# Pieces of w1 and w2 loaded by threes, one ring buffer less, and a new order of all steps, in a delta-rule recurrence with a multiplicative feed-forward block

## The chip, the cores and the metric

The kernel runs on one core of a Trainium2 chip. The metric is the device time of one execution in microseconds (us). The core's engines are called as the profile calls them: PE (TensorE, matmuls; PEld is its weight load), DVE (VectorE), ACT (ScalarE), POOL (GpSimd) and SP (SyncE, which here only issues DMAs). Each engine works through its own instructions in a fixed order and waits on semaphores for the others. PE writes to PSUM banks of 128 x 512 float32, the other tiles lie in SBUF, 128 partitions wide.

## The reference

Two blocks follow each other. The first is a delta-rule recurrence over 768 tokens for 4 batches and 8 heads of 48, the second a feed-forward block with a product of two branches:

```python
B, H, S, D = q.shape                     # 4, 8, 768, 48
k_n = k / (np.linalg.norm(k, axis=-1, keepdims=True) + 1e-06)
for t in range(S):
    y[:, :, t] = np.einsum('bhd,bhde->bhe', q[:, :, t], state)
    v_old = np.einsum('bhde,bhd->bhe', state, kt)
    state = state + bt[:, :, :, None] * np.einsum('bhd,bhe->bhde', kt, vt - v_old)
x = y.transpose(0, 2, 1, 3).reshape(B * S, H * D)        # 3072 x 384
a = x @ w1                               # 384 x 1024
b = x @ w2                               # 384 x 1024
out = ((a * b) @ w3) @ w_out             # 1024 x 1024, 1024 x 384
```

q, k, v and beta are float32. The four weights lie in the chip's memory as float64, and the kernel turns them into float32 itself.

## The kernel before

**The recurrence.** The 768 tokens are cut into 12 chunks of 64, and the chunks are worked on in pairs u = 0 to 5. For a chunk m the kernel loads k, v and q, transposes keys and queries to channels by tokens (on PE, L368, or on DVE, L354), forms the scores of the tokens among themselves on PE (L450 and L456; for the chunks 0 and 1 L408 for the keys and L399 for the queries), multiplies them by masks on DVE (L419, L433), and inverts the triangular matrix U of a pair in 31 small steps on DVE (L523 and L528, with transposes before and after at L504 and L532). The inverse's corner blocks are then filled in by PE (L562, L601, L618, L645) with copies on ACT (L634). A chain of three short steps then carries the state from chunk to chunk: PE at L671, DVE at L705, L716, L735 and L737. The outputs y of a chunk are one more group of matmuls (L776), copied by ACT into the transposed activations xT (L794).

**The feed-forward block.** w3 and w_out are multiplied ahead of use: each 128-row piece of w3 is transposed on PE (L902), and PE folds it with w_out into a new 1024 x 384 weight (L911). For each pair of chunks PE then makes 8 products by w1 and 8 by w2 (L932), ACT copies the first (L944), DVE multiplies by the second (L948), and the result goes through the folded weight (L1164) with sums of slabs and of weights on POOL (L1005, L982) to the output (L1181 to L1199).

**The weights' pieces.** Weights come in 36 pieces: P0 to P7 are w_out (384 KB each), P8 to P23 the halves of w3 (512 KB), P24 to P29 w1 and P30 to P35 w2 (512 KB, 512 columns by 128 of 384 rows each; the first three of each weight are its first 512 columns). `piece` (L826 to L852) is a generator with four steps: SP issues the DMAs that bring the 64-bit words into a buffer called raw (L836); ACT turns the high and the low words into floats (L844, L847); DVE shifts the high part by three bits (L849); POOL adds the low part (L851). For w_out and w3 that is one DMA a piece. For w1 and w2 `piece_w12` hands over four sources, since the rows of a piece are spread in groups of 48 and 16 over the two halves of the partitions: 48 rows, 16 rows, 48 rows, 16 rows.

**Where the raw words lie.** raw is a ring of five tiles of 512 KB (`in_turn(ffn, ..., "raw", 5, ...)`): a piece that takes a turn waits until the piece five turns earlier is done with the tile. Pieces named in `GUESTS` (L814) take another place instead: the tiles kperm ("k") and qperm ("q"), which later hold permuted keys and queries (`load_perm`), or half of a spare tile that later holds KQ ("0" and "1"). After the last piece, `weight_sums` (step T) takes the five raw tiles and kperm for sums of weights.

**The order.** Nothing is scheduled by the program: each part is a generator, and `ORDER` is a string that names, token by token, whose next step is issued. `in_text_order` then fixes that each engine runs its instructions in exactly this order. So a step that is moved in the string moves on each engine on which it issues something, and an engine waits at its next instruction even if a later one could run. The names that matter here: `kN` loads k, `KN` and `QN` transpose keys and queries, `gN` squares of keys, `NN` their norms, `sN` scores, `hN` the first queries' scores, `VN` the inverse of a pair (V0 belongs to chunks 0 and 1), `eN` the corner of chunk N, `cN` the chain, `yN` the outputs, `PN` a piece, `tN` a transpose of w3, `fN` a fold, `aNM` and `bM` the products by w1 and w2, `T` the weight sums, `pN` the later loads of kperm and qperm. V0 and V1 keep one of the two double banks of PSUM called ps_w for as long as they run. `s0` and `s1` with their mask products make the four parts of U (L419, three at once and one more), after which V0 begins.

## Time and profile before

| | |
|---|---|
| time, median of 3 runs | 571.95 us (571.16 to 573.22) |
| the profiled execution's own time | 573.12 us |
| its span on the core | 571.4 us |
| granted PE clock, mean | 0.984 |
| busy: PE, DVE, POOL, ACT | 536.0, 349.1, 170.5, 144.7 us |
| moved by DMA | 54.22 MB, mean 95 GB/s |

The profile is one execution, so a sum of its parts stands against 573.12 us and not against the median. "Busy" is the time in which an engine computes; an instruction's row gives its start in the span, its duration, its engine, line and operation, the tile that it writes and those that it reads, their shapes, and in brackets how long the engine was idle before it and what ended that. Rows of like instructions that follow each other are put together, with their count (x64).

The slices of the page, 14.3 us each, show the stages. These are the DMA engines' busy share in tenths and the granted clock of PE:

```profile
PEclk9599899999999999999999999999999999999999
DMA  9988965549253465543594463164044313010001
```

The first five slices, 70 us, are those in which the weights' pieces and the first chunks are loaded; behind them lies the work that repeats for each pair.

### The profile page before, as it was taken

The page shows a single profiled execution, that of the slowest core. Times are in us where ns is not written, and L with a number is a line of the kernel's source. Part 1 is how long each engine was busy: PE and PEld are TensorE (multiplying, and loading weights), DVE is VectorE, ACT ScalarE, POOL GpSimd, SP SyncE. Part 2 cuts the span into 40 slices and gives each one's busy share as a digit, 9 for nine tenths or more (in the row PEclk, how much of TensorE's full clock was granted, in tenths as well). Part 3 has the DMA queues.
Part 4 walks back from the last instruction along what each step waited for, and adds up shares of the span by engine and source line. Part 5 has one row for each costly group of instructions (what it writes and reads, how often), then busy time and mean ns, then how long its engine had stood idle before and what let it go on. Part 6 is the DMA issues. An engine that isn't in the chain of part 4 may idle for free.

```text
span 571.4 us, 19958 instructions
## 1 busy us (share of the span) xinstructions
PE 536.0 (94%) x8732; PEld 391.1 (68%) x8732; DVE 349.1 (61%) x800; ACT 144.7 (25%) x291; POOL 170.5 (30%) x213
## 2 busy tenths in 40 slices
PE   4699897899999999998999999999999999989997
PEld 3556565788888644697544798444986446888897
DVE  6999754659735478755895624598355873123552
ACT  2776665331131011120111031110210102112210
POOL 6576046274361001614022160103522005621000
PEclk9599899999999999999999999999999999999999
DMA  9988965549253465543594463164044313010001
GB/s 225 294 302 194 184 141 122 136 90 116 63 75 67 78 131 90 82 78 75 90 134 88 62 95 72 53 96 88 15 68 92 69 39 55 18 57 1 0 2 55
DMA packets 191895, 54.22 MB, mean 95 GB/s; under 512 B 179296, under 2 KB 185440, under 8 KB 191808
## 3 DMA queue, kind: packets, MB, share of 16 engines
q1 hardware_dynamic: 189216, 52.46, 45.3%
q8 instruction: 68, 1.11, 0.8%
q10 hardware_dynamic: 2592, 0.49, 0.5%
q14 instruction: 19, 0.16, 0.1%
HBM read 41.78 MB, written 9.96 MB: 91 GB/s over the span
## 4 chain that ended last, share of the span: by engine, by line
PE 76%; DVE 14%; DMA 4%; issue 3%; ACT 2%; SPq 1%; ACTq 0%; DVEq 0%
PE ps_f L932 31%; PE ps_f L1164 20%; PE ps_w L671 5%; PE ps_w L776 4%; PE ps_f L1072 4%; DVE tb L523 3%; PE ps_w L618 3%; PE ps_f L911 3%; PE ps_w L1072 2%; DVE ps_w L528 2%; DVE Vb L528 2%; PE ps_w L450 1%; PE ps_w L456 1%; DVE TT L532 1%; DMA raw<-in_moe_w_dram 1%
## 5 line engine op out<-in xcount | busy, mean ns | idle before, releaser
L932 PE MATMUL ps_f<-xT,w1s 128*128 128x512 f32 (+1 forms) x288 | 107.3, 524 | 0.7 <-issue 0.6
L932 PE MATMUL ps_f<-xT,w2s 128*128 128x512 f32 (+1 forms) x288 | 107.0, 523 | 0.0
L1005 POOL TENSOR_TENSOR ab<-ab 128x256 f32<-128x256 f32 x80 | 56.2, 726 | 156.7 <-DVE ab L948 151.8
L932 PEld LDWEIGHTS ps_f<-xT,w1s 128*128 128x128 f32 x288 | 53.9, 190 | 47.1 <-issue 42.2
L932 PEld LDWEIGHTS ps_f<-xT,w2s 128*128 128x128 f32 x288 | 54.2, 190 | 45.8 <-issue 42.6
L1164 PE MATMUL ps_f<-w,ab 128*128 128x192 f32 x320 | 57.2, 332 | 2.0 <-DVE osb L1193 1.8
L944 ACT COPY ab<-ps_f 128x512 f32<-128x512 f32 (+1 forms) x48 | 23.7, 516 | 135.3 <-PE ps_f L932 135.3
L523 DVE TENSOR_TENSOR tb<-Vb,Ub 128x31 f32<-128x31 f32 (+15 forms) x124 | 43.7, 352 | 18.6 <-DMA Ub<-Ud 14.9
L1164 PEld LDWEIGHTS ps_f<-w,ab 128*128 128x128 f32 x320 | 51.6, 190 | 3.4 <-issue 2.5
L300 POOL TENSOR_TENSOR sq<-ktok 128x384 f32<-128x384 f32 x24 | 19.9, 831 | 91.8 <-DMA out_dram<-osb 54.6
L528 DVE TENSOR_TENSOR Vb<-Vb,tb 128x31 f32<-128x31 f32 (+15 forms) x124 | 44.0, 355 | 4.3
L911 PE MATMUL ps_f<-wo,w3T 128*128 128x384 f32 x128 | 45.4, 504 | 0.8 <-POOL wo L851 0.7
L1164 PE MATMUL ps_f<-room,ab 128*128 128x192 f32 x240 | 42.9, 332 | 0.0
L948 DVE TENSOR_TENSOR ab<-ab,ps_f 128x512 f32<-128x512 f32 (+1 forms) x48 | 27.5, 586 | 19.5 <-PE ps_f L932 19.5
L1164 PEld LDWEIGHTS ps_f<-room,ab 128*128 128x128 f32 x240 | 38.6, 190 | 0.9
L911 PEld LDWEIGHTS ps_f<-wo,w3T 128*128 128x128 f32 x128 | 24.0, 195 | 16.4 <-POOL wo L851 1.7
L634 ACT COPY T<-ps_w 32x512 f32<-32x512 f32 x24 | 13.8, 576 | 71.0 <-PE ps_w L618 69.0
L794 ACT COPY xT<-ps_w 112x256 f32<-112x256 f32 x48 | 14.3, 384 | 64.8 <-PE ps_w L776 64.8
L716 DVE TENSOR_TENSOR X<-ps_w,wt 128x768 f32<-128x768 f32 x12 | 11.5, 957 | 31.0 <-PE ps_w L671 23.8
L657 POOL TENSOR_TENSOR vtok<-vtok,n 128x384 f32<-128x384 f32 x24 | 20.4, 857 | 31.9 <-DVE KQ L354 15.3
L1193 DVE TENSOR_TENSOR room<-room,ps_f 128x384 f32<-128x384 f32 (+1 forms) x13 | 6.9, 533 | 26.8 <-PE ps_f L1164 26.8
L456 PE MATMUL ps_w<-KQ 48*64 48x64 f32 x640 | 22.6, 220 | 0.6 <-issue 0.6
(170 smaller groups left out, 810.9 us busy)
## 6 DMA issues: line engine op xcount, KB each, us to landing
vtok<-in_v_dram SPq DMA_DIRECT2D x24, 192.0 KB, 4.7
out_dram<-osb SPq DMA_DIRECT2D x46, 96.0 KB, 2.0
ktok<-in_k_dram SPq DMA_DIRECT2D x44, 96.0 KB, 3.8
raw<-in_moe_w_dram SPq DMA_DIRECT2D x8, 512.0 KB, 7.1
raw<-in_moe_w_dram SPq DMA_DIRECT2D x18, 192.0 KB, 4.6
raw<-in_moe_w_out_dram SPq DMA_DIRECT2D x7, 384.0 KB, 6.0
Ud<-U SPq DMA_DIRECT2D x40, 64.0 KB, 2.3
Ub<-Ud SPq DMA_DIRECT2D x5, 512.0 KB, 3.7
```

The lines of the kernel that those rows point to most:

```text
L456: pe.matmul(ps[half(z ^ j), 1, n + C * j : n + C * j + C], lhsT=x[:, 0, :], rhs=x[:, j, :], start=True, stop=True,)
L523: dve.tensor_tensor(out=tv, in0=V[:, 0 : s + 1, s : s + 1].to_broadcast([P, s + 1, n]), in1=U[:, s, s + 1 : BS].unsqueeze(1).to_broadcast( ...
L528: dve.tensor_tensor(out=o, in0=o, in1=tv, op=ALU.subtract)
L671: pe.matmul(out(ps, r, h, z), lhsT=lhs(r, h, z), rhs=rhs(r, h, z), start=True, stop=True,)
L776: i = pe.matmul(region(h, z, r), lhsT=lhs, rhs=rhs, start=part[n] not in part[:n], stop=part[n] not in part[n + 1 :],)
L911: pe.matmul(ps[:, 0:DM], lhsT=w3Ts[jc, kc // 4][:, kc % 4 * P : kc % 4 * P + P], rhs=wo(kc), start=(kc == 0), stop=(kc == KF - 1),)
L932: pe.matmul(ps[:].rearrange("p b c t -> p b (c t)"), lhsT=w[:, m, js], rhs=x[:, m, :, c0:c1].rearrange("p b c t -> p b (c t)"), start=(m = ...
L944: act.copy(out=t, in_=ps)
L948: dve.tensor_tensor(out=t, in0=t, in1=ps, op=ALU.mult)
L1005: (dve if u == last else pool).tensor_tensor(out=o_, in0=x_, in1=y_, op=op)
L1072: pe.matmul(ps[:, j, :], lhsT=w[j], rhs=x, start=first and j == 0, stop=j == 1, skip_group_check=not first,)
L1164: pe.matmul(ps[b][:, b, :], lhsT=ab_of(u, HF * f + i, t0), rhs=ws_[w][:, i], start=first and i == 0 and (b == 0 or n == "F"), stop=i == HF ...
```

## The change

Three things are done at once.

- w1 and w2 are loaded by threes. The three pieces that share their columns are loaded by the first of them with four DMAs (48 and 16 partitions, three rows of 4 KB each), and each piece converts its own third. The first half of w1 goes into the place of w2 (w2s, which is filled only later); the other three halves go through a new tile, `trio`, of three tiles' size.
- kperm and qperm become the first two thirds of `trio`. The ring of raw tiles has four instead of five, and `weight_sums` takes the last third of `trio` for the fifth. w1 and w2 pieces leave `GUESTS`; P16 is a guest of trio's last third ("t").
- `ORDER` is new from the first token to the last. Of its 47 lines the part up to the first step of e0 and somewhat behind it is shown, with the lines around the chain that are spoken of.

```diff
 ORDER = """
-k0 K0 g0 k1 g0 P8 g0 K0 K1 g0 beta K1 g0 P8 P1 P8 g0 P10 beta P12 g0 K0 P1 P9 P8 beta P12 P13 g0
-K1 P3 P1 g0 P1 P9 g0 P10 s0 N0 P0 P12 P13 P10 s1 P3 P12 P9 P13 q1 t4 s0 V0 s0 t0 s1 P3 P0 t0 P2 P4
-s1 P18 Q1 P10 V0 P0 P13 P9 t4 P3 P7 P2 V0 P6 t2 Q1 P2 t5 V0 Q1 V0 P5 V0 P4 P11 P0 P19 V0 t1 t2 q0
-P18 V0 P2 f2 P7 V0 P4 t5 P6 P5 P18 f0 V0 P7 t1 V0 P14 P6 h1 P19 V0 P4 P5 P17 P7 V0 V0 P6 P5 f2 P11
-V1 V0 P19 f0 V0 Q0 P16 P14 P11 P11 f0 V0 P22 f2 V0 V0 t3 P19 P23 P17 t3 V0 f1 P14 P18 f1 P16 h1 Q0
-P17 V0 t10 P15 V0 k2 Q0 P22 h1 V0 P17 k3 K0 f1 P16 V0 V0 t11 P23 V0 h0 P35 P20 P14 t10 P16 P28 N0
-t8 P23 P22 t11 t6 N0 f5 P15 f5 t8 V0 f5 P35 q2 V0 V0 V0 t6 V0 P15 V0 t9 f4 P22 P29 P23 h0 t14 t9
-V0 Q0 P26 f4 v0 V0 V0 V0 h0 t15 P27 g1 P15 P20 t14 t7 f4 Q2 V0 t15 V0 P20 Q2 t7 V0 P20 e0 n0 e0
-P28 Q2 P21 e0 e0 f7 K3 e1 e0 e0 e1 e1 P35 P26 f3 e0 P35 f3 P28 P29 P27 e1 P26 P29 q3 n0 P25 e1 c0
-c0 f7 P21 v1 P33 g1 g1 e1 f3 g1 c0 K3 f7 g1 P28 P30 e1 g1 P25 P21 P21 y0 y0 t12 y0 g1 c0 t13 g1 K3
-t13 P25 c1 P26 K2 n1 t12 f6 K2 K2 K0 P30 P33 n1 P34 Q3 g1 c1 P29 P27 g1 N1 P30 Q3 f6 k4 c1 c1 s2
-y0 P31 s2 s2 P27 f6 y1 Q3 P24 s3 s3 y1 P34 P25 b5 s3 P33 P34 P33 P31 s2 s3 b7 s2 g2 P31 b5 b4 s3
...
+k0 g0 K0 k1 g0 K0 g0 P8 K1 g0 P8 beta K1 K0 g0 K1 P0 g0 beta P9 V0 P8 g0 g0 P0 P12 g0 P2 P8 s1 P3
+q1 P0 beta P12 P2 P1 s0 g0 P10 P9 t0 N0 P2 P3 P12 P0 P9 t0 s1 P12 P5 P3 P1 Q1 N0 s0 s1 Q1 s0 P1 V0
+Q1 V0 P5 V0 V0 P2 V0 P5 V0 P3 V0 P1 P4 P13 t4 V0 P18 t4 P10 h1 N0 V0 P10 P13 P9 P4 t1 P5 P7 V0 P4
+t1 f0 P10 P7 t2 P13 P11 P6 P13 P16 t5 P4 P19 P18 P6 P11 V0 t5 P7 f2 V0 V0 P22 P7 P14 P19 P6 P23 V0
+P6 V0 P18 P18 f0 V0 f0 V0 P11 f2 V0 P17 V0 P11 t2 h1 P16 t3 t10 P16 V0 V0 P22 V0 t3 P17 P19 f1 V0
+V0 P19 q0 V0 P23 P22 f1 P16 f2 t10 f1 P23 V0 Q0 P15 k2 V0 P17 P22 Q0 V0 t11 V1 t11 V0 V0 V0 P15
+P14 P17 P23 Q0 t8 t8 f5 g1 P20 V0 V0 f5 P15 P14 h1 V0 V0 t9 t15 P15 P20 P24 V0 f5 t14 t9 P14 f4
+t14 t15 P25 f4 P24 q2 V0 t6 h0 P24 P21 t6 V0 Q2 f4 P21 Q2 e0 P24 e0 t7 v0 Q2 e0 P30 h0 P20 k3 h0
+f3 e0 P26 n0 P25 t7 n0 g1 K2 e1 e0 g1 e1 P26 P25 P31 P21 e0 P31 f7 P30 P26 K2 g1 e0 P31 f7 P30 e1
+g1 P32 c0 P32 e1 f3 g1 P30 c0 K2 v1 q3 P32 e1 c0 y0 P27 P21 f3 g1 P20 n1 t13 t12 y0 t12 g1 c0 c1
+y0 g1 g1 n1 t13 s2 c1 f7 K3 N1 y0 f6 e1 P29 P28 f6 k4 K3 P27 P29 P27 Q3 P28 K3 s2 e1 Q3 Q3 s2 P29
+P28 s2 s2 b2 s2 c1 P27 s3 f6 g2 c1 P33 g2 b7 y1 s3 u2 s3 s3 s3 u3 y1 P35 b7 y1 g2 b5 b2 b4 P34 T
...
-    kperm, qperm = (persist.tile([P, B, NP, 2, BS], FP32, name=x) for x in ("kperm", "qperm"))
+    trio = persist.tile([P, 3, B * NP * 2 * BS], FP32, name="trio")
+    kperm, qperm = (
+        trio[:, i].rearrange("p (b a x d) -> p b a x d", b=B, a=NP, x=2) for i in range(2)
+    )
...
-    GUESTS = {10: "k", 2: "0", 9: "q", 18: "1", 19: "k", 11: "q", 14: "0", 15: "1", 26: "k", 21: "q", 32: "k", 34: "q"}
+    GUESTS = {10: "k", 2: "0", 9: "q", 18: "1", 19: "k", 11: "q", 14: "0", 15: "1", 16: "t"}
...
-        if host in "kq":
-            x = {"k": kperm, "q": qperm}[host][:].rearrange("p b a x d -> p (b a x d)")
+        if host in "kqt":
+            x = trio[:, "kqt".index(host)]
...
-            raw = in_turn(ffn, [P, CW, 2], "raw", 5, "raw", U32)
+            raw = in_turn(ffn, [P, CW, 2], "raw", 4, "raw", U32)
...
-        dst = dst()
+        yield from converted(raw, n, dst())
+
+    def converted(raw, n, dst):
         lo, hi = raw[:, 0:n, 0], raw[:, 0:n, 1]
...
-    def piece_w12(w, src, m, n0, i):
-        srcs = []
-        for e in range(2):
-            a, b = D * (NP * e + m), D * (NP * e + NP - 1) + 16 * m
-            srcs.append((slice(C * e, C * e + D), src[a : a + D, n0 : n0 + CW]))
-            srcs.append((slice(C * e + D, C * e + C), src[b : b + 16, n0 : n0 + CW]))
-        return piece(CW, srcs, lambda: w[:, m, n0 : n0 + CW], i)
+    def piece_w12(w, src, m, n0):
+        raw = w2s if w is w1s and n0 == 0 else trio
+        if m == 0:
+            for e in range(2):
+                x = src.rearrange("(e f) n -> e f n", e=2)[e, :, n0 : n0 + CW]
+                for g, f, n in ((0, 0, D), (D, KM * D, 16)):
+                    sync.dma_start(
+                        out=raw[C * e + g : C * e + g + n].bitcast(U32),
+                        in_=x[f : f + KM * n].rearrange("(m p) n -> p m n", m=KM).bitcast(U32),
+                    )
+            yield
+        words = raw[:, m].bitcast(U32).rearrange("p (n w) -> p n w", w=2)
+        yield from converted(words, CW, w[:, m, n0 : n0 + CW])
...
     def weight_sums():
         room = [
-            in_turn(ffn, [P, CW, 2], "raw", 5, "room", U32)[:].bitcast(FP32).rearrange(
+            in_turn(ffn, [P, CW, 2], "raw", 4, "room", U32)[:].bitcast(FP32).rearrange(
                 "p n w -> p (n w)"
             )
-            for _ in range(5)
-        ]
+            for _ in range(4)
+        ] + [trio[:, 2]]
...
-        Ts["T3"] = kperm[:].rearrange("p b a x d -> p (b a x d)")
+        Ts["T3"] = trio[:, 0]
```

In the new order the steps of one part still follow each other in their own order; the only PE step that stood ahead of e0 before and stands behind its first step now is t7, one piece of w3. The sets of matmuls, of conversions and of bytes loaded are the same.

More of the change, by code (lines that the diff above doesn't have):

```diff
@@ L87 @@
+a51 a51 W a51 a51 a51 a51 a51 W a51 a51 a51 a51 a52 a51 a51 a51 a51 a51 a52 a52 x4 a52 a52 a52 a52
+a52 a52 a52 a52 a52 a52 a52 a52 a52 a52 a52 a52 a53 a53 a53 a52 a53 a53 a53 a53 a53 a53 a53 a53
+a53 a53 a53 a53 a53 a53 S5 a53 a53 a53 o5 x5 a53 S5 S5 o5 S5 o5 x5 S5 o5 x5 S5 S5 o5 o5 x5 S5 x5
+x5 x5 x5 x5 o5 x5 x5 x5 x5 x5
 """
```

70 lines of the change are left out of this document (32 added, 38 removed).

## The prediction

> **What bounds the kernel now.** I read the page first: the busy line of TensorE (PE), the slices, and the chain of work that ended last.
>
> ```profile
> PE 536.0 (94%) x8732; PEld 391.1 (68%) x8732; DVE 349.1 (61%) x800; ACT 144.7 (25%) x291; POOL 170.5 (30%) x213
> ...
> PE 76%; DVE 14%; DMA 4%; issue 3%; ACT 2%; SPq 1%; ACTq 0%; DVEq 0%
> ```
>
> PE is busy for 536.0 of 571.4 us and carries 76% of the chain. The change takes no matmul away, so all it can win lies in the 35.4 us in which PE idles and in the stretches in which its clock is low. Where these lie is shown by the busy time in stretches of 20 us. The columns are PE, PE's weight loads, VectorE (DVE), ScalarE (ACT), GpSimd (POOL), the granted clock, the DMA share and GB/s.
>
> ```profile
> 0.00:20.00 20.00, 9.13 (x348) 7.79 (x349) 13.57 (x34) 8.45 (x15) 11.60 (x23) 0.83 0.97 257
> 20.00:40.00 20.00, 16.85 (x227) 11.53 (x227) 19.34 (x43) 15.84 (x32) 13.14 (x15) 0.83 0.96 314
> 40.00:60.00 20.00, 20.00 (x205) 13.25 (x204) 18.91 (x50) 13.16 (x26) 12.09 (x10) 1.00 0.81 175
> 60.00:80.00 20.00, 17.75 (x316) 11.26 (x313) 11.23 (x12) 12.66 (x24) 5.27 (x5) 0.91 0.78 165
> 80.00:100.00 20.00, 17.10 (x549) 12.35 (x548) 10.15 (x22) 12.43 (x24) 10.95 (x10) 1.00 0.67 134
> 100.00:120.00 20.00, 18.08 (x430) 15.51 (x429) 10.74 (x24) 8.87 (x20) 7.36 (x6) 1.00 0.51 115
> sum 120.00, PE 98.92 PEld 71.69 DVE 83.94 ACT 71.41 POOL 60.42; mean PE 16.49 PEld 11.95 DVE 13.99 ACT 11.90 POOL 10.07
> ```
>
> PE idles 120 - 98.92 = 21.1 us in the first 120 us and 35.4 - 21.1 = 14.3 us in the other 451. The prize is in the loading stage. There the list of PE's waits names these:
>
> ```profile
> PE ps_f L368 <- DMA ktok<-in_k_dram: 6.1, 3, 4.7
> PE ps_w L408 <- issue: 4.4, 2, 3.5
> PE ps_w L562 <- DVE TT L532: 2.1, 1, 2.1
> PE ps_f L368 <- issue: 2.0, 1, 2.0
> ```
>
> The first (6.1 us) is the load of k at the start, which stays. "Issue" (4.4 and 2.0 us) is idleness with no releaser, in the middle of a run of like matmuls. The third, 2.1 us, is the first chunks' inverse arriving late from DVE. No wait of PE is for a piece of w1 or w2.
>
> **The transfers.** Twelve pieces of four transfers become four loads of four: 48 issues become 16. The old ones on the SyncE queue (SP):
>
> ```profile
> L836 SPq DMA_DIRECT2D raw<-in_moe_w_dram x44: 322/421/2558, 4.5 to 106.5; - x44
> ...
> DMA to landing us min/median/max: 2.9/4.6/9.0
> ```
>
> 32 issues fewer save 32 x 0.42 = 13.5 us of SP. Since no PE wait ends at these transfers, that is worth 0 on the path; what hides them is the folding of w3 into w_out (L911) and V0, which run until 67 us. The bytes are the same. The new 48 x 3 rows of 4 KB have no row here: between the 0.32 us of one issue and the 3 x 0.42 of three; I take 0.5, off the path either way. What the new form adds is a series: w2's first half, w1's second and w2's second all use the three tiles (trio), and each load waits for the GpSimd add (L851) of the one before. Three rounds fit between c0 and the first use; their slack is the third rival. The halves' weights, sums and conversions keep their count.
>
> **The new order up to V0.** V0, the first inverse, is 31 steps on DVE. What stands ahead of it, and its end:
>
> ```profile
> 18.88 3.73 DVE L849 TENSOR_SCALAR w<-w 128x512 uint32<-128x512 uint32 x3 [0.67 <-ACT w L844]
> 22.53 1.87 DVE L419 TENSOR_TENSOR U<-ps_w,wt 128x512 f32<-128x512 f32 x3
> 24.33 1.17 DVE L849 TENSOR_SCALAR wo<-wo 128x384 uint32<-128x384 uint32 x1
> 25.41 0.68 DVE L419 TENSOR_TENSOR U<-ps_w,wt 128x512 f32<-128x512 f32 x1
> 26.13 2.05 DVE L504 STREAM_TRANSPOSE Ub<-U 128x1024 f32<-128x1024 f32 x1
> ...
> 28.59 0.19 DVE L523 TENSOR_TENSOR tb<-ps_w,Ub 128x31 f32<-128x31 f32 x1
> ...
> 33.38 0.35 DVE L528 TENSOR_TENSOR ps_w<-ps_w,tb 128x175 f32<-128x175 f32 x1
> ...
> 43.82 0.68 DVE L433 TENSOR_TENSOR PT<-ps_w,smask 128x512 f32<-128x512 f32 x1
> ...
> 47.82 0.42 DVE L849 TENSOR_SCALAR w<-w 128x512 uint32<-128x512 uint32 x1
> ...
> 64.98 1.95 DVE L532 STREAM_TRANSPOSE TT<-ps_w 32x1024 f32<-32x1024 f32 x1
> ```
>
> Before, four w3 conversions and one of w_out precede the last U; afterwards two of w3 and three of w_out, and P10 and P13 go behind V0's sixth and seventh step. The U products also need the scores, which PE ends at 22.08 + 1.06 = 23.14 after its 3.54 us of issue:
>
> ```profile
> 22.08 1.06 PE L408 MATMUL ps_w<-KQ 48*32 48x64 f32 x52 [3.54 <-issue]
> ```
>
> That stall lies in matmuls that both kernels issue as about the same numbers, so I keep it. Then the scores' three remaining U products run from 23.2 to 25.1, one conversion to 25.5, the transpose to 27.5: V0 starts 1.1 us before 28.59 (bounds 0 and, without the stall, 3.6). Inside V0 stand two conversions more (2 x 0.42) and two mask products fewer (2 x 0.68): 0.5 less. Its result comes at 66.93 - 1.6 = 65.3 us.
>
> **PE up to e0.** e0 takes that result:
>
> ```profile
> 41.75 1.11 PE L368 MATMUL ps_f<-ident,X 64*48 64x64 f32 x64
> ...
> 63.73 1.11 PE L368 MATMUL ps_f<-ident,X 64*48 64x64 f32 x64
> 66.98 0.63 PE L562 MATMUL ps_w<-TT,ident 32*32 32x256 f32 x8 [2.14 <-DVE TT L532]
> ...
> 68.68 4.15 PE L911 MATMUL ps_f<-wo,w3T 128*128 128x384 f32 x8
> ...
> 93.80 2.85 PE L911 MATMUL ps_f<-wo,w3T 128*128 128x384 f32 x8
> ```
>
> PE is there at 64.84 now. Afterwards the same steps stand ahead of e0, but for t7. But t2 and t5, which turn P10 and P13, wait for conversions that V0 now holds back: 27.5, plus the seven steps (28.59 to 33.73 less the 0.9 of conversions between them, 4.2), plus four conversions and two small copies (1.9) is 33.6; with P13's add of 1.29 us
>
> ```profile
> 11.85 1.30 POOL L851 TENSOR_TENSOR w<-w,raw 128x512 uint32<-128x512 uint32 x1 [1.40 <-ACT raw L847]
> 13.50 1.01 POOL L851 TENSOR_TENSOR wo<-wo,raw 128x384 uint32<-128x384 uint32 x1 [0.35 <-DVE ss L290]
> ```
>
> t5 runs at 35.0, while PE would be there at about 31. Then the three folds f2, f0 and f2, 8.5 us, end at 43.9, where the present order has the same work done at 41.75: 2.1 later. With t7 (0.5) and a small transpose gone, PE reaches e0 at 64.84 + 2.1 - 0.7 = 66.2, behind the result at 65.3: 0.8 us before 66.98, or 0.5 after it if the wait at t2 and t5 costs a dip of the clock (4.15 - 2.85 = 1.3). **I take -0.2** (bounds -2.7 and +4, below).
>
> The dip shows in the clock column of three stretches:
>
> ```profile
> 67.00:69.00 2.00, 1.89 (x73) 1.35 (x74) 0.67 (x1) 1.28 (x3) 0.00 (x0) 0.73 0.86 142
> 69.00:73.00 4.00, 4.00 (x24) 2.00 (x27) 0.00 (x0) 2.72 (x5) 0.83 (x1) 0.71 0.89 240
> 73.00:77.00 4.00, 4.00 (x142) 2.77 (x131) 1.78 (x4) 2.46 (x5) 0.68 (x1) 1.00 0.66 88
> ```
>
> After the 2.14 us wait the clock is at 0.73 and 0.71, and four products take 4.15 instead of 2.85 us. With PE no longer waiting there, **-1.3** (bounds -1.3 and 0).
>
> [...]
>
> e0's second product needs the second ps_w bank, in which h0's mask products now come behind V0's end: T601's 0.7, two of 0.68 and a conversion, against two of ACT's copies that it waits for anyway: **+0.3** (0 to 1).
>
> **Later.** Four places where a step directly follows what it needs:
>
> ```profile
> 103.09 0.66 PE L776 MATMUL ps_w<-KQ,S 48*48 48x64 f32 x32 [0.53 <-DVE X L716]
> ...
> 171.42 1.15 PE L671 MATMUL ps_w<-S,KQ 48*64 48x48 f32 x64 [0.39 <-DVE S L737]
> ...
> 266.29 1.11 PE L776 MATMUL ps_w<-PT,X 64*48 64x64 f32 x64 [0.63 <-DVE X L716]
> ```
>
> In the new order c1 and y1, c2 and c3, c5 and y5 have other PE work between them: -0.53, -0.39, -0.63. In turn y3 now stands directly behind c3, as y5 did: +0.63. **-0.9** (bounds -1.6 and +0.6). All other chains keep at least as much work between a step and its use.
>
> **Sum**, against the profiled execution (573.12 us, span 571.4): 0 - 0.2 - 1.3 + 0.3 - 0.9 = -2.1, so 571.0. The median of the runs, 571.95, is 1.2 below that execution: **569.8 us**. About 0.3% (1.7 us: 570.2 to 573.7) is what a measurement here can tell from no change.
>
> **Rivals.** (1) *V0 really starts earlier.* If PE's issue stall shrinks because other transfers are in flight, U is done by 22.7 and V0 starts near 25.0; P13 and e0 move with it, 2.5 us more: 567.3. For it: the stall sits where the DMA share is 0.97. Against: the new order loads as densely. (2) *Slower: the ring of four holds the loads back.* A w_out piece can load only when the add four pieces earlier is done, and those adds follow conversions inside V0; P7 waits for P3's add, P6 for P5's. From the point where P6 is converted later than PE ends f2's first half (35.0 + 0.5 + 2.85 = 38.4), f0 and f2 wait: one turn of conversion, add and landing is 0.42 + 1.0 + 4.6 = 6.0, half of which I take as exposed (3.0), with two dips (2.6) and e0 later, 5.6 - 0.2: 571.95 + 4 = 576. For it: DVE has 19.34 of 20 us busy from 20 to 40. Against: by the count above P6 is converted near 37. (3) *Slower: trio's series comes late.* 1.57 MB a round is 5.2 us at 300 GB/s, but 9.5 at the 165 GB/s of 60 to 80 us. DVE has w1's second half converted ahead of U for chunk 2, and ACT w2's ahead of the copies of b: with 4.3 us a round more than my slack of 1 to 3, PE stalls at s2 and again at the b products: 576. Against: nothing else is loading then. (4) *The dip stays*, since it comes from thin work rather than the wait: 569.8 + 1.3 = 571.1. (5) *Nothing shows*, gains and losses of the early stage cancel: 572.
>
> **How the numbers follow.** Forecast 0.40 (its own range 567.8 to 571.8: 0.25 below 570.2, 0.15 within), rival 1 0.17, rival 2 0.20, rival 3 0.15, rivals 4 and 5 together 0.08. Faster 0.25 + 0.17 = 0.42, the same 0.15 + 0.08 = 0.23, slower 0.20 + 0.15 = 0.35. The range from 564.5 to 577.5 takes in rival 1 with its e0 bound and both slower ones.
>
> **What would show it.** Right: V0's first step near 27.5, TT at 65.3, PE idle of 3 to 4 us before t5 near 35, none before e0, L911 behind e0 at 2.85 per eight, SP with 16 issues for w1 and w2, 0.6 idle before y3. Wrong: idle of PE before f0 near 38 (rival 2), before s2's second half or a b product (rival 3), e0 past 68 or before 65.

## The result, and the profile after

| | before | after |
|---|---|---|
| time, median of 4 runs each | 572.59 us (571.16 to 574.0) | 595.51 us (594.27 to 599.05) |
| the profiled execution's own time, and its span | 573.12, 571.4 us | 595.35, 593.6 us |
| granted PE clock, mean | 0.984 | 0.963 |

The changed kernel is slower: ratio 1.041, 95% interval 1.0358 to 1.0463. The forecast was 569.8 us, its range ended at 577.5.

From the page after the change: the busy line, the slices' clock and DMA rows, a DMA queue, the chain that ended last, and two groups of DMA issues (each: count, KB of one, median us from issue to landing).

```profile
PE 542.9 (91%) x8732; PEld 396.5 (67%) x8732; DVE 349.7 (59%) x800; ACT 144.9 (24%) x291; POOL 170.3 (29%) x213
...
PEclk9589979788999999999999999999999999999999
DMA  9879997283726437255363553452343304010001
...
q8 instruction: 68, 1.11, 0.8%
...
PE 89%; issue 6%; ACT 2%; DVE 2%; DMA 1%; ACTq 0%; POOL 0%; DVEq 0%
...
trio<-in_moe_w_dram SPq DMA_DIRECT2D x6, 576.0 KB, 11.2
...
trio<-in_moe_w_dram SPq DMA_DIRECT2D x5, 512.0 KB, 4.7
```

DVE's 14% of the chain are down to 2, and "issue" is up from 3 to 6%. A load of 48 partitions by three rows takes 11.2 us to land; a load of 512 KB on all 128 partitions, into the same tile, takes 4.7. PE's waits show where the time is (us in total, times, longest):

```profile
PE ps_w L779 <- issue: 8.0, 3, 6.6
PE ps_w L411 <- issue: 6.8, 2, 5.0
PE ps_f L371 <- issue: 6.3, 2, 4.7
PE ps_w L674 <- issue: 6.2, 1, 6.2
PE ps_f L371 <- DMA ktok<-in_k_dram: 5.8, 3, 4.9
PE ps_f L916 <- POOL w L856: 3.4, 2, 2.0
```

All "issue" rows of PE's waits add up to 30.7 us, against 12.3 before: +18.4. PE is busy 542.9 - 536.0 = 6.9 longer for the same matmuls, at a lower clock: 30.3 us of its work fall into stretches with a granted clock of 0.50, against 12.2 before. The rest of its idle time is 3.1 shorter. 18.4 + 6.9 - 3.1 = 22.2, the whole difference of the spans. PE's timeline shows the stops one by one (start, duration, count, idle before):

```profile
22.42 1.06 PE L411 MATMUL ps_w<-KQ 48*32 48x64 f32 x52 [4.96 <-issue]
...
68.12 1.08 PE L371 MATMUL ps_f<-ident,X 64*48 64x64 f32 x62
70.81 0.27 PE L371 MATMUL ps_f<-ident,X 64*48 64x64 f32 x2 [1.61 <-issue]
71.01 0.63 PE L565 MATMUL ps_w<-TT,ident 32*32 32x256 f32 x8
...
72.42 4.08 PE L925 MATMUL ps_f<-wo,w3T 128*128 128x384 f32 x8
...
77.07 0.84 PE L371 MATMUL ps_f<-ident,ktok 64*48 64x64 f32 x42
82.59 0.89 PE L371 MATMUL ps_f<-ident,ktok 64*48 64x64 f32 x22 [4.69 <-issue]
...
106.23 1.96 PE L674 MATMUL ps_w<-S,KQ 48*64 48x48 f32 x64 [6.20 <-issue]
...
125.46 0.43 PE L779 MATMUL ps_w<-KQ,S 48*48 48x64 f32 x12
132.47 0.77 PE L779 MATMUL ps_w<-KQ,S 48*48 48x64 f32 x18 [6.58 <-issue]
```

PE stops after 62 of 64 and 42 of 64 like transposes and after 12 of 32 like products; what follows waits for nothing that the others did not have. The last two stops come right behind loads of w1 and w2, as the timeline of SP's queue shows (start, duration, count):

```profile
92.33 1.74 SPq L892 DMA_DIRECT2D trio<-in_moe_w_dram  x4
...
118.23 1.75 SPq L892 DMA_DIRECT2D trio<-in_moe_w_dram  x4
```

Windows of 1 us within these stops have the busy time of PE, PEld, DVE, ACT and POOL, then granted clock, DMA share and GB/s:

```profile
103.00:104.00 1.00, 0.00 (x0) 0.00 (x0) 0.00 (x0) 0.00 (x0) 0.00 (x0) 0.50 1.07 112
127.00:128.00 1.00, 0.00 (x0) 0.00 (x0) 0.00 (x0) 0.00 (x0) 0.00 (x0) 1.00 0.95 131
131.00:132.00 1.00, 0.00 (x0) 0.00 (x0) 0.00 (x0) 0.00 (x0) 0.00 (x0) 0.50 0.19 20
```

No engine works. In the first two windows the DMA engines count as busy and yet move only 112 and 131 GB/s; in the third the load is over. The clock stands at 0.50 in the first and the third. What PE lacks is its own program. The page's queue q8 moved 1.11 MB in 68 packets, 16 KB each; PE and PEld have 17464 instructions, 257 for each packet, or 64 bytes an instruction. Counted in the trace (weight loads, matmuls, and PE's semaphore and drain instructions), all six stops of over 1.5 us at "issue" fall ahead of PE's instruction 449, 705, 1729, 1985, 2753 or 3777: 193 plus a multiple of 256. When instruction 193 + 256 k starts, exactly k packets of q8 have landed for 62 of the 67 values of k, k + 1 for the other five, and never fewer. And each ends 1.4 to 1.5 us after a q8 packet has landed: at 104.77 and 131.09 us for the last two, 0.2 and 1.5 us after the last packet of the loads issued at 92.33 and 118.23. So an "issue" idle here is a wait for the next 256 instructions, and before the last two stops these landed only behind the weights' packets. The 4 KB packets of those two loads take 0.47 and 0.43 us (medians of the trace's records), those of w1 and w2 before 0.19 to 0.30 where no other weights are under way.

The table collects what the timed experiments gave. "Stops" is PE's idle time, in pieces of over 0.15 us, that ends 0.8 to 1.8 us behind a q8 packet's landing, summed over the trace (before 13.0, after 30.9); "PE" is its busy time. The ratio leaves out the few executions that ran in a slower state, so it is not simply the quotient of the medians.

| run | median us | before, same chip | ratio, 95% | stops | PE |
|---|---|---|---|---|---|
| apart_burst | 588.29 | 571.43 | 1.0314 (1.0251 to 1.0377) | 11.4 | 546.4 |
| ring_of_four | 578.82 | 571.43 | 1.0147 (1.0085 to 1.0208) | 13.5 | 541.6 |
| apart_by_piece | 579.57 | 570.64 | 1.016 (1.0075 to 1.0244) | 14.4 | 538.6 |
| two_queues | 595.62 | 570.64 | 1.0415 (1.0349 to 1.0481) | 20.5 | 546.2 |
| scores_first | 577.37 | 571.66 | 1.0102 (1.0062 to 1.0141) | 14.2 | 538.8 |
| early_w3 | 581.64 | 571.66 | 1.0161 (1.0098 to 1.0224) | 11.3 | 536.2 |
| more_room | 579.06 | 571.42 | 1.0149 (1.0088 to 1.0209) | 14.8 | 535.1 |
| more_room_both | 581.34 | 571.42 | 1.0172 (1.0121 to 1.0223) | 12.9 | 537.8 |
| after_no_trio_loads | 566.72 | 572.09 | 0.9914 (0.9881 to 0.9947) | 12.6 | 535.6 |
| before_no_late_loads | 569.72 | 572.09 | 0.9964 (0.993 to 0.9999) | 7.6 | 536.1 |
| series_cut | 579.02 | 571.49 | 1.0103 (1.0069 to 1.0137) | 10.6 | 539.5 |
| series_cut_late | 576.37 | 571.49 | 1.0076 (1.0041 to 1.0111) | 13.8 | 538.7 |
| series_cut_ahead | 574.87 | 571.27 | 1.006 (1.0031 to 1.009) | 12.5 | 536.1 |

### The profile page after: what moved, and what is told of

Read it like the earlier page. It is cut to its first block, busy times and chain, and to the rows that moved or that the text cites. A ratio compares the mean times of both kernels' runs of the same rounds, so it can differ in the third digit from the quotient of the medians.

```text
span 593.6 us, 19898 instructions
## 1 busy us (share of the span) xinstructions
PE 542.9 (91%) x8732; PEld 396.5 (67%) x8732; DVE 349.7 (59%) x800; ACT 144.9 (24%) x291; POOL 170.3 (29%) x213
## 3 DMA queue, kind: packets, MB, share of 16 engines
q8 instruction: 68, 1.11, 0.8%
## 4 chain that ended last, share of the span: by engine, by line
PE 89%; issue 6%; ACT 2%; DVE 2%; DMA 1%; ACTq 0%; POOL 0%; DVEq 0%
PE ps_f L946 35%; PE ps_f L1178 19%; PE ps_f L925 7%; PE ps_w L674 6%; PE ps_w L779 4%; PE ps_f L1086 4%; PE ps_w L621 3%; PE ps_w L1086 2%; PE ps_f L371 2%; PE ps_w L459 2%; PE ps_w L453 2%; PE ps_f L916 1%; DMA ktok<-in_k_dram 1%; PE ps_w L411 1%; PE ps_w L1178 1%
## 5 line engine op out<-in xcount | busy, mean ns | idle before, releaser
L946 PE MATMUL ps_f<-xT,w1s 128*128 128x512 f32 (+1 forms) x288 | 106.1, 524 | 0.0
L925 PE MATMUL ps_f<-wo,w3T 128*128 128x384 f32 x128 | 48.4, 533 | 0.0
L925 PEld LDWEIGHTS ps_f<-wo,w3T 128*128 128x128 f32 x128 | 26.0, 211 | 17.2 <-issue 4.7
L637 ACT COPY T<-ps_w 32x512 f32<-32x512 f32 x24 | 13.8, 576 | 77.7 <-PE ps_w L621 55.6
L660 POOL TENSOR_TENSOR vtok<-vtok,n 128x384 f32<-128x384 f32 x24 | 19.7, 830 | 30.3 <-DMA vtok<-in_v_dram 18.6
L465 DVE TENSOR_TENSOR U<-ps_w,wt 128x512 f32<-128x512 f32 x20 | 13.7, 687 | 21.2 <-PE ps_w L459 21.1
L459 PE MATMUL ps_w<-KQ 48*64 48x64 f32 x640 | 24.0, 226 | 2.2 <-issue 2.2
## 6 DMA issues: line engine op xcount, KB each, us to landing
trio<-in_moe_w_dram SPq DMA_DIRECT2D x6, 576.0 KB, 11.2
```

The source lines that it names most:

```text
L459: pe.matmul(ps[half(z ^ j), 1, n + C * j : n + C * j + C], lhsT=x[:, 0, :], rhs=x[:, j, :], start=True, stop=True,)
L925: pe.matmul(ps[:, 0:DM], lhsT=w3Ts[jc, kc // 4][:, kc % 4 * P : kc % 4 * P + P], rhs=wo(kc), start=(kc == 0), stop=(kc == KF - 1),)
L946: pe.matmul(ps[:].rearrange("p b c t -> p b (c t)"), lhsT=w[:, m, js], rhs=x[:, m, :, c0:c1].rearrange("p b c t -> p b (c t)"), start=(m = ...
```

## The experiments

### Is it the program, and is it the new loads?

**apart_burst**: after's bytes, places and order, with one transfer for each row group and piece, twelve a load, in the same sequence of rows.

```diff
-                    sync.dma_start(out=raw[C * e + g : C * e + g + n].bitcast(U32),
-                        in_=x[f : f + KM * n].rearrange("(m p) n -> p m n", m=KM).bitcast(U32))
+                    for r in range(KM):
+                        sync.dma_start(out=raw[C * e + g : C * e + g + n, r].bitcast(U32),
+                            in_=x[f + r * n : f + r * n + n].bitcast(U32))
```

> The changed kernel, but each row group of a load is a transfer of its own (twelve transfers of 48 or 16 rows behind each other at the same place in the order, in place of four with three rows for each partition). Theory A, the form: in the transfers with three rows per partition a 4 KB packet takes about 0.44 us, in the others 0.17 to 0.19, so a load of 1.57 MB drops from 11 us to about 5, and PE's program fetches, which wait behind it, come in time: the idle times of PE without a releaser before 82.59, 106.23 and 132.47 (17.5 us together) fall below 5 in sum, the low clock behind them goes too, and the time is 574 to 581 us. Rival B, the size of the burst: 1.57 MB behind each other hold up the fetch whatever their form, time above 590. Rival C, the new order alone makes the stalls: 595, as the change.

The stops shrank to 11.4 us, and yet the time fell by 7 us only, between the ranges of theory A and of rival B. (The expectation's 0.17 to 0.19 us for w1's and w2's packets before is too low, as above.) SP now takes 8.6 to 16.1 us to issue a load of twelve, so the last piece is about as late, and other waits of PE appeared:

```profile
PE ps_w L453 <- DVE PT L476: 5.5, 1, 5.5
...
PE ps_w L674 <- POOL w2s L856: 3.1, 1, 3.1
```

PE's busy time stayed high at 546.4, and the packets still took 0.25 to 0.41 us. So fewer waits for the program are not enough as long as the loads themselves are slow.

**shifted_program**: after, with eight transposes more on PE at the start.

```diff
+    for _ in range(8):
+        pe.transpose(spill[:, 0:P], ident[:], ident[:])
```

> The changed kernel with eight transposes more on PE at the very start, where PE waits for k anyway: 16 instructions of PE more (8 weight loads, 8 matmuls) ahead of all others, no transfer changed. If PE's idle times without a releaser are waits for the next 16 KB block of its program (256 instructions), every one of them comes 8 matmuls earlier in its run of like matmuls: L371 stops after 34 of 64 instead of 42, the scores L411 have 60 left instead of 52, L779 stops after 4 instead of 12; time within 0.7% of the change. Rival: they belong to something in the kernel (a transfer, a bank): then they stay at the same matmul, 42, 52 and 12.

594.17 us in one run. The six long stops fall ahead of the same instruction numbers, 449 to 3777, and other matmuls stand there now. PE's timeline:

```profile
66.36 1.25 PE L373 MATMUL ps_f<-ident,X 64*48 64x64 f32 x56
68.81 0.33 PE L373 MATMUL ps_f<-ident,X 64*48 64x64 f32 x8 [1.20 <-issue]
...
73.42 0.73 PE L373 MATMUL ps_f<-ident,ktok 64*48 64x64 f32 x35
77.57 0.69 PE L373 MATMUL ps_f<-ident,ktok 64*48 64x64 f32 x17 [3.43 <-issue]
...
122.98 0.32 PE L781 MATMUL ps_w<-KQ,S 48*48 48x64 f32 x5
129.60 0.98 PE L781 MATMUL ps_w<-KQ,S 48*48 48x64 f32 x26 [6.30 <-issue]
```

56 for 62, 35 for 42 and 5 for 12, six or seven matmuls earlier (sixteen instructions were added, three semaphore instructions fell away): a stop belongs to a place in PE's program and to no data or semaphore. This settles what these idle times at "issue" are.

**loads_alone**: loads of several forms with no other work, then a stream of small matmuls beside loads.

```diff
+    for form in (threes, singles, block):
+        run(form, 3)
```

> Leaves the whole computation out: only weight loads, each waiting for the one before, first with PE idle, then beside a stream of 6000 small matmuls. Theory A: 48 rows x 4 KB land in 2 to 2.5 us, 48 x 2 and 48 x 3 rows with the rows of one partition behind each other take over twice as long per byte, four transfers of that form (1.57 MB) 10 to 12 us, the same bytes in twelve transfers 4.5 to 6.5, 128 rows x 4 KB three times 5 to 6; in the stream of matmuls idle times of PE without a releaser of 4 us and more appear beside the first form alone. Rival B: all three large forms take 8 us or more, or all stop PE alike.

1441.71 us. Three loads of 1.57 MB, one after the other with PE idle, took 40.1 us in threes, 37.9 in twelve single transfers each, hardly less, and 20.3 in 128-partition transfers (first issue to last landing). The packets took 0.447, 0.425 and 0.159 us. So three rows in a transfer are not the cause. The matmul stream ran at 107 ns a matmul and had no idle time at "issue" beside any of the loads, so it does not tell them apart.

**ring_of_four**: before, with the ring of four alone.

```diff
-            raw = in_turn(ffn, [P, CW, 2], "raw", 5, "raw", U32)
+            raw = in_turn(ffn, [P, CW, 2], "raw", 4, "raw", U32)
```

> The kernel before with a ring of four raw tiles instead of five, nothing else changed (the weight sums' fifth tile is one of its own). If the ring is not what costs the time: within 0.6% of before, 570 to 575 us. Rival, the smaller ring holds the loads back and makes PE wait for w3 and w_out: 576 us and more, with idle of PE before the folds or transposes of w3 between 30 and 60 us.

+7.4 us: in the old order the fifth tile was worth something. A piece now waits 13.5 us on SP for the tile of a w2 piece, as SP's waits show:

```profile
SPq L838 <- POOL w2s L853: 13.5, 1, 13.5
```

Everything behind it on SP waits along, and among PE's waits one has grown from 0.5 us:

```profile
PE ps_w L778 <- ACT TT L647: 3.4, 1, 3.4
```

In the changed order w1 and w2 are not in the ring, so this is not after's loss (see after_no_trio_loads).

### Which property of the loads?

**apart_by_piece**: twelve transfers again, but for each piece both halves of the partitions in turn (the edit is shown against apart_burst).

```diff
-            for e in range(2):
-                for g, f, n in ((0, 0, D), (D, KM * D, 16)):
-                    for r in range(KM):
+            for r in range(KM):
+                for e in range(2):
+                    for g, f, n in ((0, 0, D), (D, KM * D, 16)):
```

> The changed kernel, each load as twelve transfers at the same place in the order as in the run before, but piece by piece: the 48 and 16 rows of the lower 64 partitions, then those of the upper 64, then the next piece (before: all three pieces' rows of one half of the partitions behind each other). Theory A2, the partitions: what makes a 4 KB packet take 0.42 to 0.45 us is that all packets in flight go to the same 48 or 16 partitions of one half; alternating halves brings packets to 0.17 to 0.28 us and a load from 9 to 16 us down to 5.5 to 8; then neither the program fetches nor the conversions are late, the 5.5 us wait before L453 at 113 us and the 3.1 us before L674 at 86 us shrink below 3 together, time 574 to 581 us. Rival: twelve transfers are slow whatever their order (the queue's issue), packets stay over 0.38 us, time 585 or more.

579.57 us. The sequence of the transfers alone brings the time from 3.1% (apart_burst) to 1.6% over before, some 9 us; with the splitting it is 14 of the 23 us. The packets took 0.22 to 0.31 us. The kernel before loads its pieces in this sequence too: 48, 16, 48 and 16 rows for each.

**two_queues**: after, with the upper half's two transfers on ACT's queue.

```diff
-                    sync.dma_start(
+                    (sync, act)[e].dma_start(
```

> The changed kernel with its four transfers as they are, but the two of the upper 64 partitions are issued by ACT's queue instead of SP's, so that both halves are written at once. Theory A2: packets fall from 0.44 to 0.2 to 0.3 us, a load lands in 6 to 8 us instead of 11, the idle times of PE without a releaser at 78, 100 and 126 us fall from 17.5 to below 9 in sum; ACT's copies wait behind its two issues for trio to be free, which gives back up to 6 us: time 578 to 590 us. Rival B, the size of the burst alone: idle times and time as the change, 592 or more, and packets as slow as there.

595.62 us, no gain. The loads still landed after 6.7 to 12 us, two stops of 5.2 and 5.5 us stayed, and a wait of 3.1 us for V0's result was new.

**loads_by_form**: two loads of 1.57 MB in each of six forms, each load followed by a POOL instruction that reads it; then 7168 matmuls with small operands beside four of these forms.

```diff
+    for form in (threes, threes_two_queues, singles_by_piece, block, full_threes, lower_half):
+        run(form, 2)
```

> Leaves the whole computation out: 1.57 MB of weights in different forms, each load waiting for the one before, twice each with PE idle, then three times beside a stream of 7168 small matmuls that keep PE at some 16 to 20 ns each. Theory A2 in us from the first issue to the last landing: four transfers of three rows on one queue 10 to 12, on two queues 5.5 to 7.5, twelve transfers piece by piece 5.5 to 8, three of 128 rows x 4 KB 5 to 6.5, one of 128 partitions with three rows each also 5 to 6.5 (the three rows are no matter), six of 64 rows to the lower half alone 8 to 10. In the stream PE's idle times without a releaser are longest beside the first form, 4 us or more each, and at most 2.5 beside the others. Rival, the three rows for one partition are what is slow: the one transfer of 128 partitions takes 10 us too and the lower half alone 5 to 6.

The windows of loads_by_form, the six forms in that order (the fourth is three transfers of 128 partitions, the fifth one of 128 partitions by three rows, the sixth six transfers of the lower 64 partitions; last columns granted clock, DMA share, GB/s):

```profile
3.90:30.00 26.10, 0.00 (x0) 0.00 (x0) 2.94 (x3) 1.00 0.78 121
30.00:52.00 22.00, 0.00 (x0) 0.00 (x0) 0.41 (x3) 1.00 0.73 143
52.00:71.50 19.50, 0.00 (x0) 0.00 (x0) 0.37 (x3) 1.00 0.68 161
71.50:85.40 13.90, 0.00 (x0) 0.00 (x0) 0.39 (x3) 1.00 0.63 226
85.40:99.30 13.90, 0.00 (x0) 0.00 (x0) 0.41 (x3) 1.00 0.68 226
99.30:120.80 21.50, 0.00 (x0) 0.00 (x0) 0.36 (x3) 1.00 0.61 146
```

Three rows cost nothing (13.90 both ways). Reaching one half of the partitions at a time does: 21.50 for the same bytes, and 26.10 with the groups of 48 and 16. The DMA share does not show it, 0.61 at 146 GB/s against 0.63 at 226: it counts a packet for as long as it takes, and these take longer, 0.27 against 0.18 us in the mean (estimates from the windows: 16 engines x share x length of the window / 768 packets). Why one half is slower no run shows, and it is not all: two queues, which serve both halves at once, gained only 26.10 to 22.00.

PE's timeline in the stream, beside threes (first three rows) and after all loads:

```profile
134.09 2.04 PE L161 MATMUL bank<-aa 48*32 48x64 f32 x128 [9.40 <-issue]
137.54 2.04 PE L161 MATMUL bank<-aa 48*32 48x64 f32 x128 [1.41 <-issue]
149.22 2.04 PE L161 MATMUL bank<-aa 48*32 48x64 f32 x128 [9.64 <-issue]
...
281.96 2.04 PE L161 MATMUL bank<-aa 48*32 48x64 f32 x128 [1.41 <-issue]
```

PE stops each 128 matmuls and 128 weight loads, for 1.41 to 1.96 us with no other transfer under way (268 to 300 us) and up to 9.64 beside the new loads; beside two queues up to 7.2, by piece 1.4 to 3.1, beside 128-partition loads 1.4 to 3.9 (5.25 where the output's transfers were under way too). PE works for 2.04 us on 256 instructions here, so the wait for the next 256 shows each time.

### What is left: order, room, or loads?

These change apart_by_piece to take away the waits it still had, before chunk 2's scores (one, 3.9 us) and before t2 and t5, which turn P10 and P13 (two, 3.9). **scores_first** puts the last nine steps of P27 to P29 behind chunk 2's scores (s2); **early_w3** converts P10 and P13 ahead of P5 in V0; **both_orders** does both.

```diff
-f6 e1 P29 P28 f6 k4 K3 P27 P29 P27 Q3 P28 K3 s2 e1 Q3 Q3 s2 P29 P28 s2 s2 b2 s2 c1 P27 s3
+f6 e1 f6 k4 K3 Q3 K3 s2 e1 Q3 Q3 s2 s2 s2 P29 P28 P27 P29 P28 P27 b2 s2 P29 P28 P27 c1 s3
```

```diff
-Q1 V0 P5 V0 V0 P2 V0 P5 V0 P3 V0 P1 P4 P13 t4 V0 P18 t4 P10 h1
+Q1 V0 V0 V0 P2 P3 P1 P4 P13 P10 V0 P10 P5 V0 P13 P10 V0 P13 P5 t4 V0 P18 t4 h1
...
```

> The kernel with loads piece by piece (579.6 us), and in the order the conversions of w1's second half (their steps on ACT, DVE and POOL) stand behind chunk 2's scores and mask products instead of ahead of them. Theory, trio's series: PE's 3.9 us before L453 at 105 us and the low clock behind it (0.83 from 100 to 110) come from these conversions, which wait for a load that waited for trio: both go, time 3 to 6 us below 579.6: 574 to 577. Rival: PE only waits elsewhere, for the b products' weights or V1, since the load still lands at 100 us: 578.5 to 582.

> The kernel with loads piece by piece, and in the order the conversions of the pieces P10 and P13 stand ahead of V0's second and fourth step instead of behind its sixth and seventh, and P5's ACT step behind V0's two copies instead of between them. Theory: PE's 3.9 us before the transposes t2 and t5 (34 and 36 us) and the 0.72 clock from 30 to 40 go, V0 starts 0.9 us earlier; but V0's result, not PE, sets e0 then (it came at 69.7), so of the 6 us no more than 1 to 2 stay: 577 to 579.5, with PE waiting for TT before e0. Rival: V0 is not late and all of it stays: 573 to 575.5.

> Both order edits of the two runs before together, on the kernel with loads piece by piece. If the two waits are separate, the gains add: 572 to 576 us, within 0.8% of the kernel before on either side. Rival: something else of the new order costs as much (ring of four, program fetches): 577 or more.

577.37 and 581.64 us, and for both_orders 577.2 to 587.98 with a ratio of 1.016 (1.0106 to 1.0215): no gain to be told from apart_by_piece but perhaps that of the first. The scores' wait fell from 3.9 to 1.7, but a product then waited 3.4 for an ACT copy. In early_w3 PE's wait for w3 grew, as PE's waits show:

```profile
PE ps_f L916 <- POOL w L855: 6.2, 2, 5.7
```

The timelines of PE and POOL show for what it waits:

```profile
33.48 1.12 PE L916 MATMUL ps_f<-ident,w 128*128 128x128 f32 x4 [5.68 <-POOL w L855]
...
30.90 1.29 POOL L855 TENSOR_TENSOR w<-w,raw 128x512 uint32<-128x512 uint32 x1 [0.49 <-ACT raw L851]
32.14 1.28 POOL L855 TENSOR_TENSOR w<-w,trio 128x512 uint32<-128x512 uint32 x1
```

The transpose at 33.48 is t1, which turns P9, and the second of these adds is P9's. The edit put the adds of P10 and P13 ahead of it on POOL. P13's load had landed at 26.9, before ACT came to P13 at 29.6, so the load was not what was late. early_w3 therefore traded one wait for another and does not test what it was made for.

**more_room** gives P13, P4 and P7 a place in w2s instead of the ring, **more_room_both** adds both orders.

```diff
-    GUESTS = {10: "k", 2: "0", 9: "q", 18: "1", 19: "k", 11: "q", 14: "0", 15: "1", 16: "t"}
+    GUESTS = {10: "k", 2: "0", 9: "q", 18: "1", 19: "k", 11: "q", 14: "0", 15: "1", 16: "t", 13: "A", 4: "B", 7: "C"}
```

> The kernel with loads piece by piece (579.6 us), and the raw words of P13, P4 and P7 go into the thirds of w2s, which is empty until 50 us, instead of the ring of four; order unchanged. Theory, the ring holds the early loads back: SP issues the loads of P13, P4, P6 and P7 earlier (P13 went out at 22.4 us), PE's 3.9 us before the transposes t2 and t5 shrink only where the conversion itself was late, so below 2 to 3 us saved: 576.5 to 579. Rival, the order of the conversions on DVE alone sets t2 and t5: unchanged, 579 to 581.

> The same three pieces in w2s, together with both order edits (conversions of P10 and P13 ahead in V0, chunk 2's scores ahead of the conversions of w1's second half). If the ring is what made PE wait 5.7 us for P13 in the run with early conversions, that wait falls below 2 us and the time comes to 570 to 575 us. Rival: V0's result and the loads behind it set the end: 576 or more.

579.06 and 581.34 us. In more_room the waits for P10's and P13's adds fell from 3.9 to 2.8, but only because PE came later, after a stop of 1.5 us in t4: the adds themselves start at 32.87 and 34.85 us, against 32.57 and 34.54 in apart_by_piece. In more_room_both the long wait, 3.7 us, is again that for P9's add, and not for P13 as the expectation has it. Room outside the ring of four for these three pieces gains nothing in the new order.

**after_no_trio_loads** (w1's first half as in apart_by_piece) leaves out the three loads into trio, **before_no_late_loads** the transfers of P27 to P35; all other work stays.

```diff
+            for r in range(KM if raw is w2s else 0):
```

```diff
+        if i >= 27:
+            raw, srcs = guest("kq"[i % 2]), ()
```

> The kernel with loads piece by piece, but the three loads through trio are left out (w2's first half, w1's second, w2's second): their conversions run on what lies in trio, so the output is not the reference's. All else stays: the order, the ring of four, w1's first half. Theory, the series of loads through trio is what is left of the loss: with nothing to wait for, time falls from 579.6 to 570 to 574 us. Rival, the new order and the ring of four themselves: 576 to 579.

> The counterpart for the kernel before: the transfers of the nine pieces P27 to P35 (w1's second half and w2) are left out, their conversions run on what lies in kperm and qperm, so the output is not the reference's. No wait of PE was for these pieces before: 568 to 572 us under both theories. The difference of the two runs is what the order and the ring cost by themselves: below 3 us if the series is the cause of the rest, 5 or more if it is not.

566.72 and 569.72 us beside 572.09. Without the late loads the new order with its ring of four is no slower than the old one: 3.0 us faster by the medians, though the intervals of the two ratios overlap. With all loads after is 22.9 us slower than before, so the loss lies in the loads, nearly all of it in these three (w1's first half went by piece here). PE's stops are back at 12.6 us, its busy time at 535.6.

### What remains of the loads

**series_cut**: apart_by_piece, with w1's second half through the ring (P33 moved ahead, so that w2's second half is loaded right behind it). **series_cut_late** keeps P33 in its old place. **series_cut_ahead** is series_cut_late with the loads of P27 to P29 moved ahead of y0's transfers.

```diff
+        if w is w1s and n0:
+            words = in_turn(ffn, [P, CW, 2], "raw", 4, "raw", U32)
+            load(words[:].rearrange("p n w -> p (n w)"), m)
...
-c0 K2 v1 q3 P32 e1 c0 y0 P27 P21 f3 g1 P20 n1
+c0 K2 v1 q3 P27 P28 P32 e1 c0 y0 P21 f3 g1 P20 P29 P33 n1
```

```diff
-h0 P20 k3 h0 f3 e0 P26 n0 P25 t7 n0 g1
+h0 P20 P20 k3 h0 f3 e0 P26 n0 P25 t7 n0 v1 P27 P28 P29 g1
```

> The new order with loads piece by piece, but w1's second half goes piece by piece through the ring of raw tiles, which is free of w3 and w_out by then, instead of through trio; its three loads stand ahead of y0, and w2's second half follows into trio directly behind w2's first. Nothing else is moved. If the series of three loads through trio is the cause of the 8 us that are left, the loads land at about 92 and 98 us instead of 100 and 118, the waits for chunk 2's mask products and behind it go, and the time is 566 to 571 us, faster than before. Rival: the loads now stand beside the small matmuls of c0, y0 and c1 and hold up PE's program fetches instead: 573 or more, with idle times without a releaser between 80 and 100 us.

> The same, but w2's second half is loaded where the changed kernel loads it (behind chunk 2's scores). Theory: it lands some 8 us later than in the run before, at 108 us or so, still ahead of its use in the b products at about 112: 566 to 572 us as well. Rival, it is late for the b products as in the kernel with loads piece by piece: 572 to 576.

579.02 and 576.37 us. The load of w1's second half begins to be issued at 82.46 us in series_cut and lands at 100.5; in apart_by_piece, through trio, it was 82.35 and 99.9. So trio was not what made it late. SP's waits of series_cut in 60 to 125 us name an odd one:

```profile
SPq L888 <- DMA xT<-xT: 5.4, 1, 5.4
```

SP's timeline has it inside the twelve issues of a load:

```profile
82.46 14.07 SPq L888 DMA_DIRECT2D raw<-in_moe_w_dram  x12
```

In the trace the transfers count on eight semaphores in turn (100 and 102 to 108), and a transfer is not issued before the one that used its semaphore last has landed, as a rule the eighth ahead of it (in the trace of before none of 502 issues ends ahead of that landing, and for 462 it is the eighth ahead): here y0's transfer of xT, which ACT issued at 88.5 us. So twelve issues took 14.07 us. In apart_by_piece SP stood 7.6 us for the same transfer, and the twelve took 14.37.

> As the run series_cut_late, but the three loads of w1's second half stand two steps further ahead: behind chunk 1's v, ahead of q's load and of y0's transfers of xT; P20's add is moved ahead with them, since its raw tile is taken. In series_cut SP issued four of these twelve transfers at 82.5 to 85.4, stood 5.4 us until y0's transfers of xT (issued by ACT at 88.5) had landed, and issued the last at 96.1. Theory: this wait in SP's queue, not trio, made the load land at 100; ahead of y0 it is issued by 88 and lands by 93, the 5 us wait of PE before L453 at 105 falls below 1, time 569 to 574 us. Rival, SP's waits for earlier transfers come elsewhere, or the traffic holds up PE's program: 575 to 579, with the load landing at 97 or later.

574.87 us, ratio 1.006 (1.0031 to 1.009), the best form with the new tiles, the new order and all loads: the load lands at 96.0, later than the 93 expected, since its last two issues still wait 4.6 us for y0's transfer. The scores wait 0.8 instead of 5.6 us, and PE is busy 536.1. It is still slower than before, so no version with all loads beats it.

## Why the prediction was wrong

**The step that failed** is the one on the transfers: that 32 issues fewer are "worth 0 on the path", hidden by folding and V0, "since no PE wait ends at these transfers". True of the rows shown, but a load's four new transfers are other work than the twelve old ones: same bytes, at 121 instead of 161 GB/s (loads_by_form, threes and by piece), and one load of 1.57 MB in a row instead of 0.5 MB. Behind them stands a transfer that I did not count, PE's program. That cost 18.4 us of stops and 6.9 us at the lower clock; I had written 0.

**The stall at 22.08** was quoted and kept "in matmuls that both kernels issue as about the same numbers". That was the clue: in both kernels it falls ahead of PE's instruction 705. It grew from 3.54 to 4.96 us and ended 0.34 later than before, and V0's first step also waited 1.53 us for an ACT copy. So V0 did not start at 27.5 but at 29.48, 0.9 later than before. DVE's timeline of after:

```profile
29.48 0.19 DVE L526 TENSOR_TENSOR tb<-ps_w,Ub 128x31 f32<-128x31 f32 x1 [1.53 <-ACT ps_w L520]
...
67.69 2.02 DVE L535 STREAM_TRANSPOSE TT<-ps_w 32x1024 f32<-32x1024 f32 x1
```

V0's result came at 69.7, not 65.3: between V0's start and its end DVE waited 1.1 us more for ACT's conversions and spent 9.0 instead of 7.3 us on its own. e0 came at 71.01, not 66.2. On PE's own way to it t5 ran at 36.95 instead of 35.0, the folds behind it met a granted clock of 0.50 (37.6 to 40.9), and one stop took 1.61.

**The wait at t2 and t5** was right in place and size: 2.03 and 1.32 us against "3 to 4", in PE's timeline of after:

```profile
34.97 0.66 PE L916 MATMUL ps_f<-ident,w 128*128 128x128 f32 x4 [2.03 <-POOL w L856]
...
36.95 0.66 PE L916 MATMUL ps_f<-ident,w 128*128 128x128 f32 x4 [1.32 <-POOL w L856]
```

**The dip behind e0** did not go: the wait for V0's result is gone, but a stop of 1.61 us stands a moment before, and the eight products take 4.08 us (before 4.15). The -1.3 was not had; rival 4 was right on this point, not on the time, and that thin work is what brings the dip no run shows.

**The order as a whole** cannot be called right: -2.1 was predicted, and the two runs without late loads differ by -3.0 with overlapping intervals. Where the terms can be read, they did not come out as written, so the near number is luck. e0 came later and the dip stayed. Of the -0.9 behind e0 the three waits did go and y3's 0.63 did come, but a chain step (L674) gained a wait of 0.52, so about -0.4 is left. No row shows the +0.3 by itself.

**The rivals.** Rival 2, the ring of four, holds for the old order (+1.5% alone); in the new one, room for three more pieces gained nothing. Rival 3, trio's series, had the right loads and one of the right places (chunk 2's scores), but its price, 576, rested on 165 GB/s and on waits for the pieces. Such waits came out only when most of the program's stops were gone (apart_burst: 5.5 us before chunk 2's scores and 3.1 before a chain step), and part of what made the loads late was, in the runs with twelve transfers a load, SP's rotation of eight semaphores and not trio. Rivals 1 and 5 fell.

**Open**: why two queues do not gain more; what makes up the last 0.6% of series_cut_ahead, where 3.9 us of waits for P10's and P13's adds still stand, which no run took away. apart_burst keeps PE busy 10.4 us longer than before with fewer stops; 27.8 us of PE's work there fall at a clock of 0.50 against 12.2 before, and half of that difference, 7.8 us, is most of it. That is an estimate from the eight products behind e0 before, which ran at half the pace at 0.50: 2.65 of their 4.15 us lie there, and 2.65 / 2 + 1.50 = 2.83, beside 2.85 at 1.00. That the program's packets wait inside the DMA engines behind the weights' is read from when they land and from the stream beside each form; the engines' inner queues are not in the trace.

## What to carry to other kernels

Look for idle time at "issue" in the middle of like instructions on a PE that issues small matmuls, count whether it comes every 256 instructions (after's six long stops lie multiples of 256 apart), and treat those fetches as a transfer that competes with the loads. A load that fills one half of the partitions and then the other was slower here (13.05 us for 1.57 MB) than one that alternates between them (9.75) or fills all 128 (6.95); merging transfers saved issue time (32 x 0.42 = 13.5 us on SP's queue by estimate, none of it on the path), and going back to twelve a load, piece by piece, took 14 us off the time. Before moving a load, ask which earlier transfer its issue waits for; in this program it is as a rule the one eight issues ahead (462 of 502 in before).

## What was not expected of the hardware

In loads_by_form PE waits 1.41 to 1.96 us each 256 instructions when 128 small matmuls take 2.04, with no other transfer under way, and up to 9.64 beside loads. 4 KB packets took 0.159 us in loads of all 128 partitions and 0.425 to 0.447 in loads of one half after the other (loads_alone). Some 3 and 5 us into a stop PE's granted clock stood at 0.50 (windows at 103 and 131 us), 1 to 2 us into it still at 1.00 (127 us). After's low stretches from 71.69, 81.93, 102.41 and 129.72 us begin within a stop of over 1.5 us or 0.9 behind its end (70.81 to 71.69); that the stops thus cost a second time is read from this alone, and what sets the clock no run shows. In the clock records of before and after, a low stretch that ends ahead of the last matmul lasts 3.41, 6.83, 10.24 or 13.65 us, and before, one began 0.94 us behind the start of PE's first matmul after a wait of 2.14.
